# Attention and feed-forward on one core: second phase's layer 2 by seven products of block sums, weight factors partly reloaded, twelve weight halves converted early, V's low parts and the softmax sums on GpSimd

## The chip, the cores and the metric

The kernel runs on one core of one Trainium2 chip. The time is the device time of one execution in microseconds (us); the figure of a kernel is the median of its runs. Engines are named as in the profile: PE is the matrix engine (PEld its weight loads), DVE the vector engine, ACT the scalar engine, POOL GpSimd, SP the engine that issues nearly all DMA transfers.

## The reference

Block-causal attention over 8 batches of 8 heads (576 positions of width 64), followed by a two-layer feed-forward net over the 4608 tokens:

```
scores = where(block_i >= block_j, q @ k^T / 8, -1e9)       # blocks of 64 positions
attn   = softmax(scores);  x = (attn @ v) as [4608, 512]
h      = x @ w_in                                           # [4608, 2048]
g      = max(h, 0) + alpha * min(h, 0)
out    = g @ w_out                                          # [4608, 512]
```

Everything is float32 and the weights come in as float64. A float32 product is made on PE from rounded parts: each operand is split into a high part (its value in PE's float32r format) and a low part (what is left), and three matmuls (high x high, low x high, high x low) are summed in PSUM.

## The kernel before, in words

**A recorded plan.** Every operation is recorded with `op(...)` (L105): engine, an assumed cost, the buffers it reads and writes, a priority. `Plan.schedule` (L133) then runs the whole kernel once with these assumed costs and emits the instructions in the order that comes out, so each engine has one fixed queue. `SHIFTS` (L50) holds hand-set changes of single priorities. Buffers come from rooms of fixed size (`room`, L95) and from quotas by use; a buffer's next user waits until its last user is done. The eight PSUM banks are one such room.

**Attention, about the first 590 us.** There are 32 pairs of heads. `prep` (L730) loads q, k and v of a pair and splits them; from the sixth pair on (`NV` is 5, so for 27 pairs) V is kept as high and low parts: ACT makes the high parts (L764), DVE subtracts to get the low ones (L766). `query_tile` (L832) makes scores of 128 queries, their maximum on DVE, the exponential with its row sum on ACT (L875), adds the two sums of a head on DVE (L879), takes the reciprocal on DVE (L881) and scales the probabilities on POOL (L883); PE transposes them (L891), and they are split again (L970, L971). `values` (L974) multiplies with V. For the split pairs one matmul with 128 stationary columns (high and low part of V side by side) covers two of the three products, a second with 64 columns the third (L1004). The two halves of the result lie in different partitions: ACT copies one out (L1023) and DVE adds it to the other (L1025). The 576 queries of a pair are done as one span of 320 and one of 256.

**Layer work of the first phase.** The hidden width of 2048 is 16 slices of 128. The first `FA` = 6 slices are worked off in chunks of 256 tokens (`chunk_a`, L698) that fill PE between the attention's products, with ordinary products (`ffn1` L574, `ffn2` L606). The sums go to DRAM (`part`).

**Weights.** Float64 halves of a slice (w_in or w_out of 128 hidden units) are made float32 by `to_f32` (L452): one ACT and five DVE passes over 128x512. Four of the twenty halves of the last ten slices are converted during attention (`AHEAD`, L49; `weights_ahead`, L509) and kept in DRAM (`wd`), the rest behind it. `later_weights` (L524) makes, for each two slices, seven block sums of the four quarters of their w_in, split into high and low parts (all sums and low parts on POOL), and splits w_out of each slice.

**Second phase, from about 671 us.** The last ten slices are done in 9 chunks of 512 tokens. `factors` (L626) loads a chunk's x, makes seven block sums of its quarters (four sums and three low parts on DVE, four low parts on POOL). `pair1` (L649) does layer 1 of two slices as seven block products instead of eight, each six matmuls of 128x256 (L660). DVE merges the seven results in PSUM (`plus`, `onto`: L669, L673), and `activate` (L590) makes g for each of the four blocks: ACT (L593), DVE (L595), then the high part on ACT (L599) and the low part on POOL (L602). Layer 2 (`ffn2`, L606) is an ordinary product: for each slice and each 128 tokens three matmuls of 128x512 (L619) into one of four accumulating banks. `store_out` (L1112) adds each bank to the loaded first-phase sum on DVE (L1119) and stores it. So two slices of a chunk, here called a step, take 42 matmuls on L660 and 24 on L619, and there are 5 steps in a chunk and 45 in all. All weight factors of the second phase stay in SBUF.

Of the kernel before, what the change touches and what calls it, by code (L numbers as in the profile page):

```python
# [23 lines left out]
P = 128  # L24
# [13 lines left out]
BANKS, HB, AB, HT, AM, AT, WB = 6, 1, 1, 3, 2, 4, 4  # L38
# [10 lines left out]
AHEAD = {(8 + k // 2, k % 2): 12 + 4 * k for k in range(4)}  # L49
SHIFTS = {  # L50
    9: 2.6, 10: 1.7, 11: -0.8, 12: -0.5, 15: 2.4, 16: 2.1, 19: -5.7, 36: 3.1, 42: 1.1, 59: 0.6, 60: -0.7, 61: 1.4, 81.1574: 2.7, 99: -1,
    101.5278: -0.6, 119.5: 1.1, 121.8981: 0.2, 122.2685: 1.7, 153.5: 1.1, 154.5: 0.3, 155: -0.8, 155.5: 0.8, 156.5: -1.6, 175.2315: 1.4,
    180.4167: -1.6, 184.8611: -3.9,
# [4 lines left out]
B1 = 10  # L58
# [12 lines left out]
IN_ORDER = {"qraw", "kraw", "vraw", "QH", "QL", "KH", "KL", "Q", "K", "V", "raw", "m", "xb", "X", "xt"}  # L71
# [16 lines left out]
class Plan:  # L88
# [16 lines left out]
    def op(self, engine, cost, fn, r=(), w=(), prio=0.0, claim=(), then=None, ends=()):  # L105
# [3 lines left out]
        deps = {j for j, o in enumerate(self.ops) if any(b.kind in ends for b in o[4])} if ends else set()  # L109
# [14 lines left out]
        for b in bufs:  # L124
            b.users += 1
            if b.users == 1 and b.kind in IN_ORDER:
                b.after = self.last.get(b.kind)
                self.last[b.kind] = b
# [4 lines left out]
    def schedule(self):  # L133
# [31 lines left out]
        def lacks(i):  # L165
            need = {}
            for b in self.ops[i][4]:
                if b.slot is None:
                    if b.after and b.after.slot is None:
                        return b.after  # L170
                    need[b.use, b.kind] = need.get((b.use, b.kind), 0) + 1
            for (u, k), v in need.items():
                if self.quota.get(u, 0) < v:
                    return u, None
                if len(self.free.get(k, ())) < v:
                    return None, k
# [145 lines left out]
def attn_ffn(ctx, tc, qT, kT, vT, w_in, w_out, alpha, out):  # L322
# [27 lines left out]
    wd = dram.tile([2 * (NF - FA), P, 512], F32, name="wd")  # L350

# [3 lines left out]
    fa = ExitStack()  # L355
    xring = fa.enter_context(tc.tile_pool(name="xring", bufs=1))
    wa = fa.enter_context(tc.tile_pool(name="wa", bufs=1))
    xT = xring.tile([P, NCC, RING], F32, name="xT")
    fg = ctx.enter_context(tc.tile_pool(name="fg", bufs=1, side="right"))
# [91 lines left out]

    def to_f32(src, prio, after=(), use="att", early=None):  # L452

        raw, eb, fb, mb = Buf("raw"), Buf("bank", use), Buf("bank", use), Buf("m")
# [7 lines left out]
        def e():  # L462
# [14 lines left out]
            r=[raw], w=[fb], prio=prio)  # L477
# [4 lines left out]
            out=mb(), in0=mb(), scalar=2.0 ** -20, in1=eb(), op0=ALU.mult, op1=ALU.mult), r=[eb], w=[mb], prio=prio)  # L482
# [33 lines left out]

    def later(f, i, prio, after=(), use="att"):
        if (f, i) not in AHEAD:
            return to_f32((w_in, w_out)[i][f].bitcast(I32), prio, after, use)
        mb, at = Buf("m"), 2 * (f - FA) + i  # L520
        op("SP", 256, lambda: nc.sync.dma_start(out=mb(), in_=wd[at]), r=[("wd", f, i), *after], w=[mb], prio=prio)
        return mb, mb

    def later_weights(prio):  # L524


        for f in range(FA, NF, 2):
            W = w1s[f] = Buf("w1")

            ms = [later(f + i, 0, *((prio(f), ["att"], "words") if f > FA else (SOON, [], "att"))) for i in range(2)]  # L530
            (m0, w0), (m1, w1) = ms
            sb = Buf("ws")
            q11, q12 = ((m0, lambda j=j, w0=w0: w0()[:, 256 * j:256 * j + 256]) for j in range(2))
            q21, q22 = (((m1, j), lambda j=j, w1=w1: w1()[:, 256 * j:256 * j + 256]) for j in range(2))
            s1, s2 = (((sb, j), lambda j=j, sb=sb: sb()[:, 256 * j:256 * j + 256]) for j in range(2))
            pr = prio(f)
            add("POOL", 256, s1, q21, q22, ALU.add, pr, [m1, "att"])
            add("POOL", 256, s2, s1, q11, ALU.subtract, pr)
            add("POOL", 256, q21, q11, q21, ALU.subtract, pr)
# [634 lines left out]
```

## Time and profile before

| | |
|---|---|
| runs | 1123.67, 1125.45, 1126.57 us; median 1125.45 |
| profiled execution, first to last instruction (its span; the page gives no other time of it) | 1122.8 us |
| busy: PE, DVE, ACT, POOL | 99%, 74%, 64%, 55% of the span |
| instructions on PE | 7288 matmuls, as many weight loads |
| granted PE clock | 1.00 throughout |

The median lies 2.65 us above the span of the profiled execution. Busy time of an engine is the union of its instructions' durations. Instructions that follow each other on DVE overlap a little: the distance from start to start is shorter than a duration. An idle time is put down to the instruction that ended last before the waiting one began.

### The profile page before, as it was taken

How to read it: one execution, taken by the hardware profiler on the slowest of the kernel's cores; microseconds unless marked ns; L12 is line 12 of the kernel's file. 1: busy time of each engine (PE TensorE's matmuls, PEld its weight loads, DVE VectorE, ACT ScalarE, POOL GpSimd, SP SyncE). 2: the span in 40 equal slices, each digit the busy share in tenths (PEclk: the TensorE clock that was granted, in tenths of full speed). 3: DMA queues.
4: the chain of work that ended last, by engine and by line, in shares of the span. 5: the costliest groups of instructions: out<-in, count | busy, mean ns of one | idle time of the engine just before them, and what ended most of it. 6: DMA issues, size and time to landing. Idle time of an engine off the chain costs nothing.

```text
span 1122.8 us, 22035 instructions
## 1 busy us (share of the span) xinstructions
PE 1106.1 (99%) x7288; PEld 988.5 (88%) x7288; DVE 835.2 (74%) x1954; ACT 715.3 (64%) x1933; POOL 613.4 (55%) x769
## 2 busy tenths in 40 slices
PE   8999999999999999999999999999999999999998
PEld 5677989999999999999999888988988998998987
DVE  7888999888888888898857997564647465656554
ACT  7888988888888888788856655343434334343432
POOL 5767556656565556566549987243434334352422
PEclk9999999999999999999999999999999999999999
DMA  8797676576765576567324532221303030312021
GB/s 232 226 261 214 188 221 177 169 201 169 220 170 146 175 191 197 175 170 213 100 93 148 162 101 76 76 72 42 113 1 113 1 114 3 112 38 76 2 75 38
DMA packets 75314, 147.96 MB, mean 132 GB/s; under 512 B 9792, under 2 KB 11840, under 8 KB 75200
## 3 DMA queue, kind: packets, MB, share of 16 engines
q1 hardware_dynamic: 74768, 146.28, 44.4%
q8 instruction: 58, 0.95, 0.4%
q14 instruction: 56, 0.46, 0.1%
q10 hardware_dynamic: 432, 0.27, 0.1%
HBM read 68.40 MB, written 29.36 MB: 87 GB/s over the span
## 4 chain that ended last, share of the span: by engine, by line
PE 85%; DVE 7%; ACT 3%; POOL 2%; issue 2%; DMA 1%; SPq 0%; DVEq 0%; ACTq 0%; POOLq 0%
PE bank L619 33%; PE bank L660 19%; PE bank L582 11%; PE bank L1004 6%; PE bank L859 5%; PE bank L891 5%; PE bank L994 2%; PE bank L921 2%; PE bank L947 1%; ACT p L875 1%; DVE xh L568 1%; PE bank L854 1%; DVE PL L971 1%; DVE g L595 1%; POOL p L883 1%
## 5 line engine op out<-in xcount | busy, mean ns | idle before, releaser
L602 POOL TENSOR_TENSOR gl<-g,gh 128x256 fp32r<-128x256 f32 x288 | 220.0, 772 | 309.6 <-PE bank L660 173.5
L660 PEld LDWEIGHTS bank<-X,w 128*128 128x128 f32 x1890 | 253.7, 189 | 20.6 <-POOL X L488 1.2
L660 PE MATMUL bank<-X,w 128*128 128x256 f32 x1890 | 259.2, 281 | 0.6 <-POOL X L488 0.5
L619 PE MATMUL bank<-w,gh 128*128 128x512 f32 x720 | 225.7, 395 | 1.1 <-DVE g L669 0.7
L883 POOL TENSOR_SCALAR p<-p,ri 128x512 f32<-128x512 f32 (+3 forms) x256 | 153.0, 611 | 115.7 <-DVE ri L881 45.5
L593 ACT ACTIVATE g<-bank 128x256 f32<-128x256 f32 x288 | 110.7, 386 | 155.1 <-DVE bank L673 138.0
L599 ACT CAST gh<-g 128x256 fp32r<-128x256 f32 x288 | 117.0, 407 | 85.2 <-DVE g L595 84.0
L595 DVE SCALAR_TENSOR_TENSOR g<-g,oal,bank 128x256 f32<-128x256 f32 x288 | 136.0, 475 | 42.0 <-ACT g L593 36.6
L673 DVE TENSOR_TENSOR bank<-bank,g 128x256 f32<-128x256 f32 x180 | 76.1, 428 | 104.7 <-PE bank L660 103.2
L875 ACT ACTIVATE p<-bank,nm 128x512 f32<-128x512 f32 (+3 forms) x256 | 135.0, 532 | 20.9 <-DVE nm L872 6.9
L619 PE MATMUL bank<-w,gl 128*128 128x512 f32 x360 | 141.6, 393 | 0.0
L619 PE MATMUL bank<-wa,gh 128*128 128x512 f32 x432 | 140.0, 405 | 0.0
L619 PEld LDWEIGHTS bank<-w,gh 128*128 128x128 f32 x720 | 120.3, 188 | 14.2 <-DVE g L669 0.9
L582 PE MATMUL bank<-xh,wa 128*128 128x256 f32 x864 | 131.2, 287 | 0.4 <-DVE xh L568 0.4
L971 DVE TENSOR_TENSOR PL<-bank,PH 128x512 fp32r<-128x512 f32 (+2 forms) x189 | 111.8, 608 | 12.6 <-ACT PH L970 10.3
L582 PEld LDWEIGHTS bank<-xh,wa 128*128 128x128 f32 x864 | 114.8, 190 | 3.2 <-DVE xh L568 1.1
L891 PE MATMUL bank<-ident,p 128*128 128x128 f32 x640 | 109.4, 276 | 4.7 <-POOL p L883 3.2
L859 PE MATMUL bank<-K,Q 128*128 128x512 f32 (+1 forms) x472 | 104.2, 331 | 0.3 <-ACT p L875 0.2
L970 ACT CAST PH<-bank 128x512 fp32r<-128x512 f32 (+2 forms) x189 | 97.0, 529 | 11.0 <-PE bank L891 7.3
L669 DVE TENSOR_TENSOR g<-bank,g 128x256 f32<-128x256 f32 x135 | 56.8, 422 | 49.1 <-PE bank L660 47.8
L891 PEld LDWEIGHTS bank<-ident,p 128*128 128x128 f32 x640 | 75.3, 140 | 18.6 <-POOL p L883 8.3
L619 PE MATMUL bank<-wa,gl 128*128 128x512 f32 x216 | 85.5, 396 | 0.3 <-POOL gl L602 0.2
(124 smaller groups left out, 2016.7 us busy)
## 6 DMA issues: line engine op xcount, KB each, us to landing
Q<-QH SPq DMA_DIRECT2D x62, 256.0 KB, 3.8
K<-KH SPq DMA_DIRECT2D x124, 128.0 KB, 3.7
vraw<-in_v SPq DMA_DIRECT2D x32, 320.0 KB, 3.1
qraw<-in_q SPq DMA_DIRECT2D x31, 320.0 KB, 3.8
xd<-xT SPq DMA_DIRECT2D x8, 1152.0 KB, 5.7
part<-o SPq DMA_DIRECT2D x36, 256.0 KB, 3.2
xb<-xd SPq DMA_DIRECT2D x9, 1024.0 KB, 5.3
m<-part SPq DMA_DIRECT2D x36, 256.0 KB, 3.3
```

What stands on the lines that cost most here:

```text
L582: nc.tensor.matmul(hp()[:, :n], ww()[:, 0, cc * P:(cc + 1) * P], x()[:, cc, :n], start=(i == 0 and cc == 0), stop=(i == 2 and cc == NCC - 1))
L593: op("ACT", c_act(CHA), lambda: nc.scalar.activation(out=g(), in_=hp()[:, ts], func=AF.Relu, scale=-1.0), r=[hp], w=[g], prio=FP)
L595: op("DVE", c_dve(CHA) + 60, lambda: nc.vector.scalar_tensor_tensor(out=g(), in0=g(), scalar=oal[:, f:f + 1], in1=hp()[:, ts], op0=ALU.mul ...
L599: op("ACT", c_act(CHA, True), lambda: nc.scalar.copy(out=gh(), in_=g()), r=[g], w=[gh], prio=FP)
L602: op("POOL", c_pool(CHA), lambda: nc.gpsimd.tensor_tensor(out=gl(), in0=g(), in1=gh().bitcast(F32), op=ALU.subtract), r=[g, gh], w=[gl], p ...
L619: nc.tensor.matmul(acc(), a()[:, ts], ww(), start=(first and i == 0), stop=(last and i == 2))
L660: nc.tensor.matmul(bank()[:, :CHA], W()[:, i, 256 * at + P * c:256 * at + P * c + P], B()[:, j, CHA * c:CHA * c + CHA], start=(n == 0), st ...
L859: nc.tensor.matmul(o, Q()[:, i, qs], K()[:, 2 * h + i, :w], start=(i == 0), stop=(i == 1))
L875: op("ACT", 238 + w / 1.2, lambda h=h, t=t: nc.scalar.activation(out=t()[:, :w], in_=sb[h]()[:, off[h]:off[h] + w], func=AF.Exp, bias=nm() ...
L883: op("POOL", 244 + w / 1.2, lambda h=h: nc.gpsimd.tensor_scalar(out=pts[h]()[:, :w], in0=pts[h]()[:, :w], scalar1=ri()[:, h:h + 1], scalar ...
L891: nc.tensor.transpose(out=tp()[:, base + c * P:base + (c + 1) * P], in_=pts[h]()[:, c * P:(c + 1) * P], identity=ident)
L971: op("DVE", c_dve(n) + (HALF if n == P else 0), lambda: nc.vector.tensor_tensor(out=lo(), in0=src(), in1=hi().bitcast(F32), op=ALU.subtrac ...
```

## The change

**Layer 2 of the second phase.** `pair2` takes the place of `ffn2` there. For two slices and 256 tokens, the 2x2 blocks of g (two slices by two times 128 tokens) and of w_out (two slices by two times 256 columns) are multiplied with seven block products, each three matmuls of 128x256. g is not split any more when it is made (`activated` writes it to one half of a buffer `G` of 512). Instead `pair2` splits three of its blocks (ACT and POOL, 128x384), makes four block sums in place on DVE (one instruction over two blocks, two over one block each) and splits four blocks (ACT and POOL, 128x512). Four banks take the seven products over all five steps, and `store_out` then merges them with the first-phase sums in seven DVE and four POOL additions of 128x256 and one ACT copy, for 256 tokens. w_out gets block sums and split factors like w_in (`factors_of`); the sums are on DVE now, and of the four low parts of a set two are on DVE and two on POOL.

**Room.** The factors of w_in of four of the five slice pairs (`STREAMED`) share two buffers: each is written to DRAM once (`wq`) and loaded again, 1792 KB, for each of the eight later chunks: 32 loads. Buffers of several kinds now share rooms (x factors, g factors and the first phase's weights; G, x sums and loaded sums). The accumulating banks and the waiting layer-1 results are given more of the eight banks.

**First phase.** Twelve halves instead of four are converted during attention. V's low parts (L766 before) and the addition of the two softmax sums (L879 before) are on POOL. For the span of 256 queries (`LIGHT`) the product of 128 stationary columns becomes two of 64, so all six matmuls of a head end in the same partitions: an ACT copy to xT ends it, and the DVE addition (L1025 before) and the copy L1023 are gone there.

`SHIFTS` is set anew; it is cut below. The order of the changed kernel counts 108 more matmuls of attention (the 108 with 128 stationary columns in the spans of 256 become 216 with 64), 1890 of 128x256 for layer 2 in place of 1080 of 128x512, and 128 sums and 54 low parts of V more on POOL.

Three places in the order. The first is PE in the second phase, in the middle of a chunk. Before (X are x factors, w weight factors, gh and gl the parts of g):

```order
L619 MATMUL bank_181<-w_7878,gh_8159 128x512 x2
L619 MATMUL bank_181<-w_7878,gl_8186 128x512
L660 MATMUL bank_222<-X_7991,w_8230 128x256 x6
L660 MATMUL bank_241<-X_7995,w_8230 128x256 x6
L660 MATMUL bank_188<-X_8118,w_8230 128x256 x6
L619 MATMUL bank_203<-w_8027,gh_520 128x512 x2
L619 MATMUL bank_203<-w_8027,gl_549 128x512
```

In the changed kernel (L705 is layer 1, L785 layer 2; wa are the factors of x and of g, wr a reloaded and w a resident set of weight factors):

```order
L705 MATMUL bank_226<-wa_826,wr_7807 128x256 x6
L705 MATMUL bank_249<-wa_1075,wr_7807 128x256 x6
L785 MATMUL bank_237<-w_8449,wa_7638 128x256 x2
L785 MATMUL bank_237<-w_8449,wa_804 128x256
L785 MATMUL bank_189<-w_7689,wa_370 128x256 x2
L785 MATMUL bank_189<-w_7689,wa_1069 128x256
L705 MATMUL bank_226<-wa_873,wr_7807 128x256 x6
```

All products are now of one size, and a layer-2 product reads factors that ACT, POOL and DVE have made from sums of g.

The second place is DVE in the second phase. Before (u or g are merged results, L595 the activation):

```order
L595 SCALAR_TENSOR_TENSOR g_7465<-g_7465,oal,bank_188 128x256
L673 TENSOR_TENSOR bank_241<-bank_241,g_7445 128x256
L595 SCALAR_TENSOR_TENSOR g_7426<-g_7426,oal,bank_241 128x256
L673 TENSOR_TENSOR bank_222<-bank_222,g_8074 128x256
L669 TENSOR_TENSOR g_7495<-bank_188,g_8074 128x256
```

In the changed kernel (L774, L776, L777 are the block sums of g; L713 and L717 the merges, L725 the activation, L1241 the merge of the sums of layer 2):

```order
L713 TENSOR_TENSOR u_8262<-bank_249,u_8260 128x256
L713 TENSOR_TENSOR u_8099<-bank_237,u_8260 128x256
L774 TENSOR_TENSOR raw_168<-raw_168 128x2x128
L717 TENSOR_TENSOR bank_237<-bank_237,u_8262 128x256
L776 TENSOR_TENSOR raw_168<-raw_168 128x128
L717 TENSOR_TENSOR bank_189<-bank_189,u_8099 128x256
L777 TENSOR_TENSOR raw_168<-raw_168 128x128
L725 SCALAR_TENSOR_TENSOR m_324<-m_324,oal,bank_237 128x256
L1241 TENSOR_TENSOR m_7606<-bank_226,m_7606 128x256
```

Between the merges, which read one operand from a PSUM bank, there now stand sums with both operands in SBUF. One chunk has 106 DVE instructions: 49 merges from PSUM and 20 activations, 30 block sums of g, 4 sums and 3 low parts of x.

The third place is PE in attention, the value product of one head over 256 queries. Before:

```order
L1004 MATMUL bank_181<-PH,V_1236 128x256
L1004 MATMUL bank_181<-PL,V_1236 64x128
L1004 MATMUL bank_181<-PL,V_1236 64x256
L1004 MATMUL bank_181<-PH,V_1236 128x128
```

In the changed kernel:

```order
L1101 MATMUL bank_143<-PH,V_1224 64x256
L1101 MATMUL bank_143<-PH,V_1224 64x128
L1101 MATMUL bank_143<-PH,V_1224 64x256
L1101 MATMUL bank_143<-PH,V_1224 64x128
L1101 MATMUL bank_143<-PL,V_1224 64x256
L1101 MATMUL bank_143<-PL,V_1224 64x128
```

A head has six matmuls there for four.

The diff, cut:

```diff
-AHEAD = {(8 + k // 2, k % 2): 12 + 4 * k for k in range(4)}
+AHEAD = {(10 + k // 2, k % 2): 6 + 2 * k for k in range(12)}
+ON = "DVE", "DVE", "POOL", "DVE", "POOL"
+VLO, SUMS, LIGHT = "POOL", "POOL", (256,)
+STREAMED = (6, 8, 12, 14)
...
 SHIFTS = {
-    9: 2.6, 10: 1.7, 11: -0.8, 12: -0.5, 15: 2.4, 16: 2.1, 19: -5.7, 36: 3.1, 42: 1.1, 59: 0.6, 60: -0.7, 61: 1.4, 81.1574: 2.7, 99: -1,
+    9: 1.6, 11: -0.8, 15: 2.4, 25.5: 2.4, 36: 3.1, 61: 1.4, 63.5: 3.6, 65: -1.3, 66.713: 6, 68.1944: -0.2, 70.0463: 2.5, 72: -1.4, 73.5: -5,
...
+    def factors_of(key, W, m0, m1, sums, pr):
...
+        for to, x, y, f in sums[:3]:
+            to, x, y = ((*q, *t)[k] for k in (to, x, y))
+            add(ON[0], 256, to, x, y, f, pr, [b0, b1, "att"])
+        for src, r, at, n in ((w0, [b0, "att"], 0, 512), (w1, [b1], 2, 512), (lambda: sb(), [t[0][0], t[1][0]], 4, 512)):
...
+            split(src, hi, lo, n, [*r, *[(r[0], j) for j in range(2) if at < 4]], ((*key, at), "h"), ((*key, at), "l"), [W], ON[1 + at // 2], pr)
...
+    def weights_of(f):
...
+        W = Buf("wr")
+        op("SP", 1792, lambda: nc.sync.dma_start(out=W().rearrange("p a b -> p (a b)").bitcast(F32), in_=wq[STREAMED.index(f)]),
+           r=[("wq", f)], w=[W], prio=0)
...
+    def pair2(f, G, accs, turn, tail):
...
+        def parts(j, n, src):
+            op("ACT", c_act(n * T, True), lambda: nc.scalar.copy(out=at(0, j, n), in_=src()), r=gk, w=[(F[0], j)], claim=F, prio=turn)
+            on = "DVE" if j and tail else "POOL"
...
+        parts(0, 3, lambda: g(1, 3))
+        op("DVE", c_dve(2 * T), lambda: nc.vector.tensor_tensor(out=blocks(2, -2 * T), in0=blocks(0, 0), in1=blocks(2, -T), op=ALU.subtract),
+           w=gk, prio=turn)
+        op("DVE", c_dve(T), lambda: nc.vector.tensor_tensor(out=g(1), in0=g(1), in1=g(2), op=ALU.subtract), w=gk, prio=turn)
+        op("DVE", c_dve(T), lambda: nc.vector.tensor_tensor(out=g(3), in0=g(3), in1=g(1), op=ALU.subtract), w=gk, prio=turn)
+        parts(3, 4, lambda: g(0, 4))
...
+                for n, (x, y) in enumerate(((0, 0), (0, 1), (1, 0))):
+                    nc.tensor.matmul(accs[bank]()[:, 256 * half:256 * half + 256], at(x, j), W()[:, y, w:w + 256],
+                                     start=(first and n == 0 and not half), stop=(last and n == 2), skip_group_check=True)
...
-                op("DVE", c_dve(n), lambda cs=cs: nc.vector.tensor_tensor(
+                op(VLO, c_pool(n) if VLO == "POOL" else c_dve(n), lambda cs=cs: (nc.gpsimd if VLO == "POOL" else nc.vector).tensor_tensor(
...
+            if SUMS == "POOL":
+                op("POOL", 130, lambda: nc.gpsimd.tensor_tensor(out=sp(), in0=s()[:, :, 0], in1=s()[:, :, 1], op=ALU.add),
...
+                if q1 in LIGHT:
+                    prods = [(x, c) for c, _ in cs for x in ("h", "m", "l")]
...
+    def store_out(accs, t):
...
+        op("ACT", c_act(256), lambda: nc.scalar.copy(out=u1(), in_=acc(0)), r=[accs[0]], w=[u1], prio=FP)
+        plus(lambda: half(ohi, 0), lambda: acc(1), lambda: half(ohi, 0), [accs[0]], [(ohi, 0)])
+        plus(lambda: half(ohi, 0), lambda: half(ohi, 0), u1, [u1], [(ohi, 0)], "POOL")
+        plus(u2, lambda: acc(3), u1, [accs[1], u1], [u2])
...
     fs = range(FA, NF, 2)
-    for t0 in range(0, TOK, CHB):
+    for c, t0 in enumerate(range(0, TOK, CHB)):
         X = factors(t0)
...
+        gs = [pair1(f, X, base + L1T * i) for i, f in enumerate(fs)]
+        for k in range(2):
+            accs = [Buf("bank", "acc") for _ in range(4)]
+            for i, f in enumerate(fs):
...
+                pair2(f, gs[i][k], accs, turn2, t0 + CHB == TOK)
+            store_out(accs, t0 + CHA * k)
```

252 lines of the change are left out of this document (161 added, 91 removed), and 8 rows, old and new, of the table SHIFTS.

## The prediction

> **What bounds the kernel now.** First the page's totals, the granted clock and the chain that ended last.
>
> ```profile
> PE 1106.1 (99%) x7288; PEld 988.5 (88%) x7288; DVE 835.2 (74%) x1954; ACT 715.3 (64%) x1933; POOL 613.4 (55%) x769
> ...
> PEclk9999999999999999999999999999999999999999
> ...
> PE 85%; DVE 7%; ACT 3%; POOL 2%; issue 2%; DMA 1%; SPq 0%; DVEq 0%; ACTq 0%; POOLq 0%
> ```
>
> PE is idle for 1122.8 - 1106.1 = 16.7 us and always at full clock, so a gain needs less PE work, and a loss needs an engine that makes PE wait. The windows (PE, PEld, DVE, ACT, POOL busy, clock, DMA share, GB/s) show where the others stand.
>
> ```profile
> 200.00:300.00 100.00, 99.83 (x720) 92.88 (x719) 88.19 (x226) 83.85 (x243) 61.45 (x82) 1.00 0.67 187
> ...
> 650.00:670.00 20.00, 18.95 (x120) 16.46 (x120) 19.96 (x41) 10.68 (x27) 17.24 (x18) 1.00 0.23 75
> ...
> 700.00:800.00 100.00, 100.00 (x627) 89.88 (x626) 57.97 (x125) 39.93 (x99) 41.03 (x47) 1.00 0.19 64
> ```
>
> In attention DVE at 88% costs PE 0.2%. Behind it, while weights are made, DVE is busy 99.8% of 20 us and PE loses 1.05 us, 5%. In the second phase DVE and POOL have room. The chain of waits gives PE's prices there (start, time, what).
>
> ```profile
> 700.04 2.79 PE bank L619 x12
> 702.84 2.12 PE bank L660 x18
> ...
> 710.57 2.81 PE bank L619 x12
> ```
>
> 2.79/12 = 0.2325 us for 512 columns, 2.12/18 = 0.1178 for 256. A step is 24 x 0.2325 + 42 x 0.1178 = 10.53 us, just what lies between the starts at 700.04 and 710.57: nothing but matmuls fill it.
>
> **Layer 2 by seven products.** It takes 1080 x 0.2325 = 251.1 us now and will take 1890 x 0.1178 = 222.6: -28.5 us. The price is that of layer-1 products, which have the same form. A chunk of 512 tokens is then 420 x 0.1178 = 49.5 us of PE, for 52.7.
>
> **The value products.** One head over 256 queries, from PE's timeline:
>
> ```profile
> 304.90 0.28 PE L1004 MATMUL bank<-PH,V 128*128 128x256 f32 x1
> 305.02 0.34 PE L1004 MATMUL bank<-PL,V 128*64 128x128 f32 x2
> 305.19 0.23 PE L1004 MATMUL bank<-PH,V 128*128 128x128 f32 x1
> 305.25 0.83 PE L891 MATMUL bank<-ident,p 128*128 128x128 f32 x6
> ```
>
> From start to start the 256-wide one takes 0.12 us and the 128-wide one 0.06. Two more are added: 0.18 x 54 = +9.7 us, on PE, which is full there, so all of it counts. That the halved weight loads give something back would show as short intervals behind the 64-column ones, and 305.02 to 305.19 (0.17 for 256 and 128) shows none.
>
> **Engines in attention.** The groups by form (busy, mean ns):
>
> ```profile
> L766 DVE TENSOR_TENSOR V<-vraw,V 128x384 fp32r<-128x384 f32 x27 | 17.3, 642 | 3.5 <-ACT V L764 3.2
> L766 DVE TENSOR_TENSOR V<-vraw,V 128x256 fp32r<-128x256 f32 x27 | 12.5, 463 | 0.0
> L879 DVE TENSOR_REDUCE sp<-s 128x2 f32<-128x4 f32 x128 | 19.1, 150 | 11.1 <-ACT p L875 9.9
> L1025 DVE TENSOR_TENSOR xT<-bank,tmp 64x256 f32<-64x256 f32 x54 | 22.6, 418 | 2.9 <-ACT tmp L1023 1.9
> L478 DVE SCALAR_TENSOR_TENSOR m<-raw,bank 128x512 f32<-128x512 uint32 x32 | 21.6, 679 | 0.0
> L570 POOL TENSOR_TENSOR xl<-xT,xh 128x384 fp32r<-128x384 f32 x8 | 8.3, 1047 | 1.1 <-DVE xh L568 0.7 <-PE bank L582 0.4
> L602 POOL TENSOR_TENSOR gl<-g,gh 128x256 fp32r<-128x256 f32 x288 | 220.0, 772 | 309.6 <-PE bank L660 173.5 <-ACT gh L599 123.0 <-PE bank L619 10.3
> L883 POOL TENSOR_SCALAR p<-p,ri 128x128 f32<-128x128 f32 x64 | 28.2, 451 | 11.0 <-DVE ri L881 6.8 <-ACT KH L746 1.1 <-ACT xT L1012 1.1
> ```
>
> DVE loses 17.3 + 12.5 + 19.1 + 22.6 = 71.5 us and gets eight more conversions, 8 x 5 x 0.68 = 27. POOL gets 27 x (1.05 + 0.77) = 49 us of low parts and 128 sums. A sum of 128x2 is not in the trace on POOL: between 0.15 us (DVE's, with nothing for POOL's start) and 0.45 (its 128x128 form); I take 0.25, so 32 us. POOL goes from about 60% to 75% over some 580 us, DVE down to about 80%. Both stay below what DVE carries at 88% now: zero in the sum. The sum waits in POOL's queue behind a low part of up to 1 us, and behind it wait the reciprocal, the scaling and the transposes; chunk work of the first phase fills PE meanwhile. Without that cover it would be 128 x up to 1 us. A gain on PE is excluded by its 99.8%. The sixteen DMAs of eight conversions (512 KB in, 256 KB out) meet a DMA share of 0.67: nothing.
>
> **Engines in the second phase.** This decides. The price of POOL's wide forms and of DVE's narrow one, and DVE's timeline in a stretch where POOL runs without a break, then POOL's own:
>
> ```profile
> L488 POOL TENSOR_TENSOR w<-m,w 128x512 fp32r<-128x512 f32 x20 | 26.3, 1318 | 3.3 <-ACT w L487 3.3
> L971 DVE TENSOR_TENSOR P<-bank,P 64x128 fp32r<-64x128 f32 x27 | 7.7, 284 | 1.7 <-ACT P L970 0.8
> ```
>
> ```profile
> 736.97 1.11 DVE L488 TENSOR_TENSOR X<-xt,X 128x512 fp32r<-128x512 f32 x1
> 738.00 0.47 DVE L595 SCALAR_TENSOR_TENSOR g<-g,oal,bank 128x256 f32<-128x256 f32 x1
> 738.39 0.41 DVE L669 TENSOR_TENSOR g<-bank,g 128x256 f32<-128x256 f32 x1
> 738.72 1.06 DVE L504 TENSOR_TENSOR xt<-xb,xt 128x512 f32<-128x512 f32 x1
> 739.70 1.23 DVE L488 TENSOR_TENSOR X<-xt,X 128x512 fp32r<-128x512 f32 x1
> ...
> 750.34 0.68 DVE L488 TENSOR_TENSOR X<-xb,X 128x512 fp32r<-128x512 f32 x1
> 750.94 0.88 DVE L673 TENSOR_TENSOR bank<-bank,g 128x256 f32<-128x256 f32 x2
> ```
>
> ```profile
> 736.23 3.00 POOL L488 TENSOR_TENSOR X<-xb,X 128x512 fp32r<-128x512 f32 x2 [1.83 <-ACT X L487]
> 739.20 1.18 POOL L602 TENSOR_TENSOR gl<-g,gh 128x256 fp32r<-128x256 f32 x1
> 740.34 1.74 POOL L488 TENSOR_TENSOR X<-xb,X 128x512 fp32r<-128x512 f32 x1
> ```
>
> Start to start, DVE takes 0.39 us for an activation, 0.33 for a 256-wide merge, 0.60 for a 512-wide sum (750.34 to 750.94). But a DVE instruction with both operands in SBUF takes 0.68 us alone and 1.11, 1.06 and 1.23 while POOL works: 0.45 us longer on average. POOL is slowed as well (1.74 for 1.32). A merge with one operand in PSUM (738.39) is not.
>
> POOL per chunk: ten splits of 384 and ten of 512, eight additions, four low parts of x: 10 x 1.05 + 10 x 1.32 + 8 x 0.77 + 4 x 1.32 = 35.2 us, 71% of 49.5. DVE per chunk: 49 x 0.33 + 20 x 0.39 + 10 x (0.33 + 0.28 + 0.28) + 7 x 0.60 = 37.1 us. Of these, 37 instructions have both operands in SBUF; at 0.45 x 0.71 = 0.32 us each they wait 11.8 us. DVE comes to 48.9 us, 99% of PE's time. ACT has 0.39 of its time in use and trades four splits of 256 for two pairs of wider ones: no bound.
>
> By the Trainium skill (SBUF — State Buffer, Who interferes with whom) the two engines share a port that the second comer does not get until the first one's instruction ends, when a DVE instruction has two SBUF inputs and POOL reads SBUF. The trace agrees: 1.23 us against 0.68.
>
> So the change spends nearly all of DVE's room. The cost to PE lies between nothing and the 5% of the window with DVE at 99.8%: 0 to 23 us of 446. I take 7, nearer the lower end, since products of both layers fill in for each other and PE lost only 0.2% at 88%.
>
> **The making of the weights.** Eight conversions fewer stand behind attention (-27 us of DVE); ten sets of sums and low parts on DVE, 10 x (4 x 0.33 + 2 x 0.60) = +25 us, and their six SBUF instructions wait on POOL, up to 60 x 0.32 = 19 us. POOL is freed: five sets of 0.77 x 4 + 1.32 x 3 + 0.77 and ten single splits of 1.32, 52 us, become 10 x (1.32 + 0.77) = 21. Between -1 and +8 us on PE (5% of the 150 us in question); I take +1.
>
> **Reloads.** 32 loads of 1792 KB. From the page's issues:
>
> ```profile
> xb<-xd SPq DMA_DIRECT2D x9, 1024.0 KB, 5.3
> m<-part SPq DMA_DIRECT2D x36, 256.0 KB, 3.3
> ```
>
> The 768 KB between these cost 2.0 us, so 1792 KB land in 5.3 + 2.0 = 7.3 us, or 9.3 in proportion to the larger. In the order 87 to 102 matmuls, 10.3 to 12.0 us, stand between the last use of the old set and the first of the new for half the loads, some 20 us for the rest. They are hidden: zero.
>
> **The end.** The last 256 tokens need a POOL addition (0.77) behind DVE's, and whole stores instead of halves: +1.2 us.
>
> Sum: -28.5 + 9.7 + 7 + 1 + 1.2 = -9.6 us. The span goes from 1122.8 to 1113.2; with the 2.65 us between the span and the median of the runs, 1115.8. Without any new wait it would be 1107.8, with the 23 us it would be 1131.8.
>
> **The rivals.** *DVE becomes the bound* (slower). If the mean wait of the 37 instructions passes (49.5 - 37.1)/37 = 0.335 us, DVE and not PE sets the chunk. POOL's instructions get longer (1.05 and 1.32 for 0.77), and half of one is 0.59 us; times 0.71 that is 0.42, so 52.6 us a chunk, +3.1 x 9 = 28 us instead of 7: 1137. At 0.45, POOL always busy, it is 53.8 and 1147. For it: the sums are back to back with waits on each other, so POOL's next instruction can slip in between each two. Against it: 0.32 is below the point, and in attention a DVE nearly as full costs nothing. By the rule of the Trainium skill quoted above (SBUF — State Buffer, Who interferes with whom) the wait is the rest of POOL's instruction, and the time that of this rival.
>
> *The making of the weights stalls PE.* The DVE work there grows by up to 17 us net; if PE pays 8, the time is 1123, no change. For it: DVE is at 99.8% there already. Against: POOL's 31 us less.
>
> *The reloads come late* (slower). If they land after 12.5 us, because x, sums and stores share the queues, 16 of them cost 1.5 us each: +24, 1140. Against: 10.5 MB a chunk (four reloads, x, sums, stores) in 49.5 us is 212 GB/s, and the window at 200 us moves 187 at a share of 0.67 with smaller packets.
>
> *The saving is not there*, because the products of layer 2 don't run at 0.1178: the count is set by the order and the form is that of layer 1, so this is unlikely.
>
> **How the numbers follow.** A measurement can tell about 0.3% (3.4 us) from no change: faster is below 1122.1, slower above 1128.8. Forecast 0.57 (own range 1107 to 1123), DVE as the bound 0.24, weights 0.11, reloads 0.06, no saving 0.02. Faster: 0.54 of the forecast and 0.05 of the weights, 0.59. Same: 0.03, 0.05 of the weights, 0.06 of the milder cases of DVE, 0.14. Slower: the rest, 0.27. The range goes from 1106 to 1142: it leaves out DVE's upper cases (0.08), half the reloads (0.03) and little below.
>
> **What would show it.** Right: layer 2 at 0.118 us a matmul and PE at 98% or more in the second phase; DVE near full there, with the sums of g (128x2x128) lengthened to 0.6 us or more; chunks 50 to 51 us apart. Attention longer by 10 us. Wrong: chunks 52.5 us or more apart with PE waiting for DVE or POOL (the rival), PE waiting for a DMA into wr (reloads), PE below 95% between 600 and 750 us (weights).

## The result, and the profile after

| | before | after |
|---|---|---|
| median of the runs | 1125.85 us (1123.67 to 1126.57, 4 runs) | 1185.22 us (1183.0 to 1185.7, 4 runs) |
| ratio | | 1.0529, 95% interval 1.0514 to 1.0544 |
| span of the profiled execution | 1122.8 us | 1181.2 us |

The change costs 59 us; 9.6 us of gain were forecast. The page of the changed kernel:

```profile
PE 1110.8 (94%) x8206; PEld 1027.7 (87%) x8206; DVE 972.7 (82%) x2147; ACT 732.7 (62%) x1961; POOL 762.6 (65%) x983
...
PEclk9999999999999999999999979999999999999999
...
PE 64%; DVE 23%; issue 5%; ACT 3%; POOL 3%; DMA 1%; SPq 0%; POOLq 0%; DVEq 0%; ACTq 0%
```

PE is busy about as long as before, but the chain runs through DVE for 23% of the span, not 7%, and one slice of the clock is below 9. The windows tell where (PE, PEld, DVE, ACT, POOL busy, clock, DMA share, GB/s; in parentheses the instructions):

```profile
200.00:300.00 100.00, 97.87 (x720) 91.09 (x721) 80.70 (x185) 84.24 (x245) 70.67 (x115) 1.00 0.71 206
597.00:653.00 56.00, 55.75 (x354) 50.60 (x355) 50.40 (x83) 30.77 (x70) 37.27 (x35) 1.00 0.56 209
653.00:713.00 60.00, 43.45 (x289) 39.47 (x288) 58.32 (x108) 29.03 (x67) 31.03 (x27) 0.86 0.49 171
713.00:773.00 60.00, 53.51 (x420) 51.41 (x420) 51.96 (x109) 23.09 (x54) 36.30 (x33) 0.97 0.47 176
773.00:1046.00 273.00, 259.17 (x2159) 255.49 (x2158) 235.80 (x541) 117.36 (x279) 179.40 (x165) 1.00 0.55 202
1096.00:1181.00 85.00, 70.78 (x564) 67.71 (x564) 66.47 (x146) 27.45 (x65) 40.24 (x41) 0.99 0.28 103
```

Read PE's column against the length of each row. Attention is nearly full. In the first chunk of the second phase, while weights are still made, PE stands for 16.6 of 60 us beside a DVE that is busy for 58.3. In the steady chunks (773 to 1046) all products are 256 wide, so the count of matmuls tells the loss: 2159 x 0.1178 = 254.3 us of work in 273, 18.7 us or 6.8% lost, although DVE is busy for only 86%.

The whole by stages. "Lost" is the length of a stage less its matmuls at 0.2325 or 0.1178 us each; the stages are cut at the first layer-1 product of a chunk.

| | before | after | difference |
|---|---|---|---|
| first layer-1 product of the second phase | 641.8 | 653.0 | +11.2 |
| lost in chunks 1 and 2 | 3.2 | 35.5 | +32.3 |
| lost in chunks 3 to 8 | 0 | 25.8 | +25.8 |
| lost in chunk 9 | 0 | 13.4 | +13.4 |
| behind the last matmul | 3.7 | 5.4 | +1.7 |
| work of PE (what is left) | | | -26.0 |
| span | 1122.8 | 1181.2 | +58.4 |

What works on DVE and POOL in the steady chunks, by form (busy us, mean ns of one | idle before it). The group rows here and below are of 773 to 1070 us, the window rows of 773 to 1046; the sums that use the second buffer (`raw`, 15 of each) are rows of their own and are left out:

```profile
L717 DVE TENSOR_TENSOR bank<-bank,u 128x256 f32<-128x256 f32 x111 | 44.7, 421 | 7.7 <-ACT m L723 4.3 <-PE bank L705 3.5
L774 DVE TENSOR_TENSOR m<-m 128x256 f32<-128x256 f32 x41 | 30.0, 732 | 4.7 <-POOL wa L771 4.7
L776 DVE TENSOR_TENSOR m<-m 128x128 f32<-128x128 f32 x41 | 23.6, 576 | 0.4
L777 DVE TENSOR_TENSOR m<-m 128x128 f32<-128x128 f32 x41 | 17.5, 427 | 0.4
L771 POOL TENSOR_TENSOR wa<-m,wa 128x512 fp32r<-128x512 f32 x40 | 52.9, 1325 | 49.2 <-ACT wa L769 41.3 <-issue 4.1 <-PE bank L705 2.3
```

The merge with one operand in PSUM (L717) and the block sum with both in SBUF (L774) have one size: 0.42 and 0.73 us. The two smaller sums differ by 0.15 us though they are the same instruction. POOL has its price of before (1.32) and is idle for 49 us before these low parts, 41 of them for ACT. ACT in turn waits for DVE's last sum, and PE for DVE's activation (us, times, longest), in the same stretch:

```profile
POOL wa L771 <- ACT wa L769: 68.1, 41, 4.0
ACT wa L769 <- DVE m L777: 58.9, 26, 4.8
...
PE bank L705 <- DVE m L725: 6.8, 6, 1.6
```

The chain of waits inside a steady chunk (start, time, what) is a row of DVE instructions, and the lengthened sums stand in it:

```profile
850.15 0.52 ACT wa L769
850.99 0.87 DVE m L725 x2
851.86 0.34 DVE bank L717
852.20 0.89 DVE m L774
853.11 1.14 DVE m L776
```

Of the other steps, the reloads and what attention gave to POOL:

```profile
wr<-wq SPq DMA_DIRECT2D x32, 1792.0 KB, 7.3
```

```profile
L859 POOL TENSOR_TENSOR V<-vraw,V 128x384 fp32r<-128x384 f32 x27 | 27.4, 1013 | 24.4 <-ACT V L857 20.4 <-DMA K<-KH 3.5 <-POOL sp L973 0.3
L973 POOL TENSOR_TENSOR sp<-s 128x2 f32<-128x2 f32 x128 | 25.6, 203 | 50.6 <-ACT p L968 50.2
```

No DMA into wr stands among PE's waits. A sum of 128x2 costs POOL 0.20 us.

### The profile page after: what moved, and what is told of

Same layout as the page of the kernel before. It is cut to its first block, busy times and chain, and to the rows that moved or that the text cites. A ratio compares the mean times of both kernels' runs of the same rounds, so it can differ in the third digit from the quotient of the medians.

```text
span 1181.2 us, 24258 instructions
## 1 busy us (share of the span) xinstructions
PE 1110.8 (94%) x8206; PEld 1027.7 (87%) x8206; DVE 972.7 (82%) x2147; ACT 732.7 (62%) x1961; POOL 762.6 (65%) x983
## 4 chain that ended last, share of the span: by engine, by line
PE 64%; DVE 23%; issue 5%; ACT 3%; POOL 3%; DMA 1%; SPq 0%; POOLq 0%; DVEq 0%; ACTq 0%
PE bank L624 12%; PE bank L661 10%; PE bank L705 9%; PE bank L785 9%; PE bank L1101 7%; PE bank L952 6%; PE bank L988 5%; DVE bank L717 2%; DVE u L713 2%; DVE m L774 2%; DVE m L519 2%; PE bank L1091 2%; PE bank L1018 2%; DVE m L776 1%; POOL wa L771 1%
## 5 line engine op out<-in xcount | busy, mean ns | idle before, releaser
L785 PE MATMUL bank<-w,wa 128*128 128x256 f32 x1890 | 269.6, 285 | 19.7 <-POOL wa L771 9.2
L785 PEld LDWEIGHTS bank<-w,wa 128*128 128x128 f32 x1890 | 243.8, 191 | 25.4 <-POOL wa L771 12.6
L705 PE MATMUL bank<-wa,wr 128*128 128x256 f32 x1512 | 215.1, 285 | 24.9 <-DVE m L725 12.2
L705 PEld LDWEIGHTS bank<-wa,wr 128*128 128x128 f32 x1512 | 195.2, 192 | 30.8 <-DVE m L725 14.5
L771 POOL TENSOR_TENSOR wa<-m,wa 128x384 fp32r<-128x384 f32 (+1 forms) x125 | 148.1, 1195 | 104.6 <-ACT wa L769 91.0
L980 POOL TENSOR_SCALAR p<-p,ri 128x256 f32<-128x256 f32 (+3 forms) x256 | 140.7, 562 | 34.8 <-DVE ri L978 30.6
L968 ACT ACTIVATE p<-bank,nm 128x256 f32<-128x256 f32 (+3 forms) x256 | 134.1, 530 | 23.2 <-DVE nm L965 11.8
L644 POOL TENSOR_TENSOR gl<-g,gh 128x256 fp32r<-128x256 f32 x108 | 86.2, 798 | 50.0 <-ACT gh L641 43.2
L1067 ACT CAST PH<-bank 128x512 fp32r<-128x512 f32 (+2 forms) x189 | 96.9, 528 | 17.2 <-PE bank L988 12.9
L965 DVE TENSOR_REDUCE nm<-bank 128x1 f32<-128x384 f32 (+1 forms) x128 | 76.7, 616 | 11.1 <-PE bank L952 9.9
L1101 PE MATMUL bank<-PH,V 128*128 128x320 f32 (+3 forms) x432 | 85.1, 289 | 0.0
L771 POOL TENSOR_TENSOR wa<-raw,wa 128x384 fp32r<-128x384 f32 (+1 forms) x45 | 54.4, 1213 | 44.7 <-ACT wa L769 36.1
L717 DVE TENSOR_TENSOR bank<-bank,u 128x256 f32<-128x256 f32 x180 | 71.9, 422 | 13.2 <-PE bank L705 7.2
```

What stands on the lines that cost most here:

```text
L705: nc.tensor.matmul(bank()[:, :CHA], W()[:, i, 256 * at + P * c:256 * at + P * c + P], B()[:, j, CHA * c:CHA * c + CHA], start=(n == 0), st ...
L771: op(on, c_pool(n * T) if on == "POOL" else c_dve(n * T), lambda: (nc.gpsimd if on == "POOL" else nc.vector).tensor_tensor(out=at(1, j, n) ...
L785: nc.tensor.matmul(accs[bank]()[:, 256 * half:256 * half + 256], at(x, j), W()[:, y, w:w + 256], start=(first and n == 0 and not half), st ...
L968: op("ACT", 238 + w / 1.2, lambda h=h, t=t: nc.scalar.activation(out=t()[:, :w], in_=sb[h]()[:, off[h]:off[h] + w], func=AF.Exp, bias=nm() ...
L980: op("POOL", 244 + w / 1.2, lambda h=h: nc.gpsimd.tensor_scalar(out=pts[h]()[:, :w], in0=pts[h]()[:, :w], scalar1=ri()[:, h:h + 1], scalar ...
L1067: op("ACT", c_act(n) + (HALF if n == P else 0), lambda: nc.scalar.copy(out=hi(), in_=src()), r=rk, w=[(*k, 0) for k in wk], prio=pr)
```

## The experiments

Theory A, formed after the result: a DVE instruction with two SBUF operands waits for POOL's running instruction; these waits lengthen the chain from g to the factors in every chunk, and fill DVE while the weights are made. Rival B: the longer chain itself (activation, split, sums, split) is too long for the order, waits or not. Rival D: the reloads. All times below stand against runs of the kernel before on the same chip (1124.3 to 1125.1 us). The first four experiments keep the order of the changed kernel. In all others it is made anew, with the `SHIFTS` that were set by hand for the changed kernel, so a part of their differences can be the order's.

**One SBUF input for the sums of g.**

```
-tensor_tensor(out=g(1), in0=g(1), in1=g(2), op=ALU.subtract)
+tensor_reduce(out=g(1), in_=g(1) with an axis of 1, axis=AX.X, op=ALU.add)     # and so for all three
```

> The three block sums of g in pair2 (L774, L776, L777) are replaced by DVE passes of the same length in the same order that read one operand from SBUF instead of two, so that they don't ask for what POOL holds; the subtraction is left out, so layer 2 multiplies other numbers. Nothing else moves. Theory A (DVE's two-input instructions wait for POOL, and these waits delay the factors): these instructions fall to 0.42 and 0.28 us each, the six steady chunks lose 1 us instead of 4.3, the last 80 us lose half, 1185 becomes about 1150. Theory B (the chain merge, activation, split, three sums, split is too long and DVE too full even without waits): 1178 to 1190, chunks still 53 us apart.

Measured: 1147.0 us (ratio 1.0199, 1.0169 to 1.0228), 38 less than the changed kernel. The windows, then the groups of the steady chunks:

```profile
653.00:773.00 120.00, 101.64 (x740) 96.24 (x739) 105.56 (x221) 55.55 (x129) 70.57 (x63) 0.90 0.51 184
773.00:1046.00 273.00, 272.04 (x2301) 271.03 (x2301) 218.06 (x585) 125.86 (x298) 188.46 (x177) 1.00 0.58 217
```

```profile
L775 DVE TENSOR_REDUCE m<-m 128x128 f32<-128x128 f32 x88 | 23.1, 275 | 0.0
L775 DVE TENSOR_REDUCE m<-m 128x256 f32<-128x256 f32 x44 | 18.0, 410 | 2.1 <-POOL wa L771 2.1
```

The subtraction is left out; the order, the sizes and POOL's work are the same. 0.41, 0.275 and 0.275 us stand where 0.73, 0.58 and 0.43 stood, and PE loses 273 - 2301 x 0.1178 = 1.9 us instead of 18.7. B falls. The Trainium skill (SBUF — State Buffer, Who interferes with whom) says that a tensor_reduce never contends with GpSimd on trn2, and that at most one SBUF input, outside DVE's 2-port modes, keeps DVE off the shared port; these rows agree.

**The same for all sums and for DVE's low parts of x and of the weights** (not for the low parts of g that DVE makes in the last chunk).

> As the run before, and also the sums of x and of the weights and the low parts that DVE makes read one SBUF operand only, in the same order (subtractions left out). Theory A: the waits are gone everywhere, the 35 us lost between 653 and 773 us fall below 12, total about 1120. Theory B: as without this, 1175 to 1190. Theory C (behind attention DVE has simply too much to do to make the weights in time, waits or not): the chunks behind 773 us get as in the run before, but 25 us or more stay lost between 653 and 773 us, total 1135 to 1150.

Measured: 1122.56 us (ratio 0.9976, 0.9965 to 0.9987).

```profile
653.00:773.00 120.00, 113.77 (x914) 111.33 (x913) 99.01 (x269) 62.96 (x149) 79.19 (x76) 0.97 0.63 228
773.00:1046.00 273.00, 273.00 (x2321) 273.00 (x2320) 210.50 (x583) 128.23 (x300) 184.83 (x177) 1.00 0.57 208
```

The steady chunks are now full, and chunks 1 and 2 lose 10.8 us instead of 35.5. So the waits are worth 62.7 us of 1185, and without them the change would just about break even. The run takes POOL's waits for DVE away as well; they are small, since POOL's low parts of g shrink only from 1.33 to 1.30 us (512 columns) and from 1.07 to 1.02 (384). In chunks 1 and 2 the sums of g alone (the run before) bring 4.8 of the 24.7 us, the sums and low parts of the weights and of x the rest. Theory C of this expectation (DVE has too much to do there, waits or not) falls: 10.8 us are lost, not 25 or more.

**The other side of the conflict: little work for POOL.** The low parts of g's factors on 16 columns:

```
-out=at(1, j, n), in0=src(), in1=at(0, j, n)
+out=at(1, j, n)[:, :16], in0=src()[:, :16], in1=at(0, j, n)[:, :16]
```

> The low parts of g's factors (384 and 512 columns) are written for 16 columns only, the rest is left out; every other instruction and the order stay. This takes GpSimd's side of the conflict away and leaves VectorE's sums with their two SBUF operands. Theory A (VectorE waits for GpSimd's instruction to end): GpSimd falls from 65% to some 30% of the steady chunks, the sums from 0.73, 0.58 and 0.43 us to at most 0.50, 0.38 and 0.35, and the chunks lose 0-1 us: 1130-1150 us. Rival W (the sums are long of themselves, because they read and write one buffer in place): 0.73, 0.58 and 0.43 us stay, and the time falls only by what the shorter GpSimd instructions take out of the chain: 1160-1180 us.

Measured: 1142.96 us (ratio 1.0159, 1.0143 to 1.0175). Window and groups of the steady chunks:

```profile
773.00:1046.00 273.00, 270.42 (x2289) 269.65 (x2288) 222.96 (x582) 123.83 (x293) 86.35 (x175) 1.00 0.57 211
```

```profile
L774 DVE TENSOR_TENSOR m<-m 128x256 f32<-128x256 f32 x43 | 22.9, 532 | 0.0
L776 DVE TENSOR_TENSOR m<-m 128x128 f32<-128x128 f32 x43 | 14.5, 338 | 1.7 <-DVE m L774 0.5
L777 DVE TENSOR_TENSOR m<-m 128x128 f32<-128x128 f32 x44 | 13.5, 306 | 0.4
```

The sums are unchanged in code, yet take 0.53, 0.34 and 0.31 us with POOL busy for 32% instead of 66%. So their length is POOL's doing; rival W falls. (L774 stays 0.03 us above what was expected at most.) This run shortens the chain as well, so its time alone would not tell A from B; the durations do.

**Reloads of 64 bytes** in each partition instead of the whole set:

```
-dma_start(out=W()..., in_=wq[...])
+dma_start(out=W()...[:, :16], in_=wq[...][:, :16])
```

> The 32 reloads of weight factors move 16 of the 3584 words of each partition; issues, waits and order stay (the factors of the reloaded sets are mostly those of another slice). Theory D (reloads come late or their traffic slows others): 15 us faster or more. Theories A, B and C: within 4 us of 1185, since PE's waits in the trace name DVE, POOL and ACT, and the reloads land in 7.3 us.

Measured: 1184.46 us (ratio 1.0532, 1183.94 to 1184.98 us): no change. D falls.

**A version with the whole computation and no wait at the sums of g.** ACT copies g into a PSUM bank, and each sum reads one operand there:

```
+op("ACT", ..., nc.scalar.copy(out=C(), in_=g(0, 4)), r=gk, w=[C], claim=F)       # C = Buf("bank", "gp"), one
-tensor_tensor(out=g(1), in0=g(1), in1=g(2), op=ALU.subtract)
+tensor_tensor(out=g(1), in0=c(1), in1=g(2), op=ALU.subtract)                     # and so for all three
```

> Before the three block sums of g, ScalarE copies g into one PSUM bank (one more buffer, taken from the eight) and each sum reads one of its two operands there: one SBUF input for each of the three, the computation whole. Theory A (time lost to VectorE's waits): the sums take 0.40-0.45 and 0.28 us instead of 0.75, 0.57 and 0.41, the steady chunks lose 0-2 us instead of 4.3, and the weights stage loses less: 1145-1162 us. Rival L (what counts is the length of the chain from g to the factors, whoever makes it long): the copy adds 0.6 us to a chain from which 0.76 us of waits go, and one bank fewer holds the merges: 1172-1190 us.

Measured: 1158.26 us (ratio 1.0296, 1.028 to 1.0311). Window and groups of the steady chunks:

```profile
773.00:1046.00 273.00, 266.00 (x2203) 261.65 (x2202) 216.64 (x560) 144.17 (x332) 184.18 (x168) 1.00 0.56 203
```

```profile
L783 DVE TENSOR_TENSOR m<-bank,m 128x256 f32<-128x256 f32 x40 | 16.8, 420 | 4.7 <-ACT bank L782 2.8 <-POOL wa L771 1.1
L786 DVE TENSOR_TENSOR m<-bank,m 128x128 f32<-128x128 f32 x41 | 11.8, 287 | 0.9
L785 DVE TENSOR_TENSOR m<-bank,m 128x128 f32<-128x128 f32 x41 | 11.7, 285 | 0.5
```

The sums are as short as A said, with POOL as busy as ever (184 of 273), and 27 us come back. But 2203 x 0.1178 = 259.5: the steady chunks still lose 13.5 us of 273. The time lies in A's range, but two thirds of what the waits cost there are still lost, some 2.5 us a chunk, above A's 0-2. So rival L is right in part: the length of the chain counts too. Which costs more, the copy in the chain, the bank less or the new order on ACT and DVE, was not separated.

**Who makes the weights.** First all on POOL (`ON` five times "POOL"):

> All block sums of the weights and all their low parts on GpSimd, as the kernel before had them; the plan is made anew. In the changed kernel VectorE is busy 58.3 of the 60 us from 653 to 713, and the first two chunks of the second phase lose 35.5 us of TensorE's time. Theory A (VectorE, stretched by its waits for GpSimd, sets the pace while the weights are made): some 28 us of VectorE's instructions leave 597 to 773 and about 32 us come onto GpSimd, which was busy 67 of the 120 us there: the loss falls to 10-20 us, 1165-1178 us. Rival C (the number of sums and splits is too much for either engine in this time): GpSimd is over 90% busy in that stretch and the loss stays at 30 us or more, 1180-1200 us. The six steady chunks lose their 25 us under both.

Measured: 1192.35 us (ratio 1.0596, 1.058 to 1.0612).

```profile
653.00:713.00 60.00, 28.21 (x196) 26.20 (x195) 20.21 (x42) 24.18 (x53) 59.69 (x63) 0.76 0.49 170
```

Now POOL is full (59.7 of 60) and PE stands for 32 us. Rival C's marks came true (chunks 1 and 2 lose 39.5 us): giving DVE's part back only changes which engine is full. That the work is too much for either engine holds for POOL; DVE, freed of its waits, could do it in time (the run with all sums on one input). Then, on top of the PSUM copy, the low parts of both raw halves on POOL, where one of them and that of the last sum are already; the block sums and the low parts of the first two sums stay on DVE (`ON = "DVE", "POOL", "POOL", "DVE", "POOL"`):

> The PSUM copy of g, and the weights' work split between the two engines: block sums and the low parts of the sums on VectorE, the low parts of the raw halves on GpSimd; the computation whole. In the version with the PSUM copy alone VectorE is busy 55.6 of the 60 us from 653 to 713 and GpSimd 32.8; with all on GpSimd it is 59.7 against 20.2. Theory A with C (whichever engine is full sets the pace of the making, and the sum of both leaves room): about 45 us on each, the two first chunks lose 4-9 us instead of 14: 1148-1155 us. Rival (the order of the conversions and the DMA, not an engine, sets the pace): no change, 1156-1162 us.

Measured: 1157.78 us (ratio 1.0294, 1.0275 to 1.0312), no change to the PSUM copy alone.

```profile
653.00:713.00 60.00, 44.01 (x304) 39.85 (x302) 55.79 (x106) 33.07 (x75) 46.08 (x37) 0.91 0.50 174
```

My 45 us on each engine did not come: POOL rises to 46.1 while DVE stays at 55.8, now for 106 instructions (with the PSUM copy alone 55.6 us for 112): what is left on DVE takes longer beside a busier POOL. The rival's range (1156 to 1162) holds the time; the split is not the cure. The 14 us of my expectation were wrong as well: counted as in the table above, chunks 1 and 2 lose 27.8 us with the PSUM copy alone and 23.9 here, and 3.0 of these 3.9 us go again because the second phase starts later.

**Early conversions undone**: four halves in attention, as many as before (`for k in range(4)` in `AHEAD`; slices and places are not those of the kernel before).

> Four weight halves converted early in attention, as the kernel before had it, not twelve; the other eight are converted between attention and the second phase; the plan is made anew. Theory A with C (VectorE is full while the weights are made: 160.7 of the 176 us from 597 to 773): eight conversions are 32 VectorE instructions of 0.68 us, 22 us, which come on top of that; attention ends some 0-4 us earlier, the second phase's first two chunks lose 45-60 us instead of 35.5: 1192-1210 us. Rival R (the early conversions are what makes attention longer, and the later place has room): attention's last product by 592 us instead of 597.4, no more lost behind it: 1176-1186 us.

Measured: 1198.32 us (ratio 1.066, 1.0632 to 1.0688). Attention's last product is at 593.6 us instead of 597.4; chunk 3 begins at 786.2 instead of 773.3. The early conversions cost attention about 4 us and have saved 13 on balance by chunk 3; chunks 1 and 2 lose 47.8 us without them. That is what A with C expected.

**Attention.** `LIGHT = ()`, so the span of 256 is multiplied as before:

> LIGHT is emptied: value products, copies and additions of the spans of 256 as before the change, the order planned anew. By the prediction's term PE has 9.7 us less to do in attention; if the 64-column products also cause the 7 us that PE loses there (it waits for ACT copies behind them), attention ends 15 to 17 us earlier, total 1168 to 1172; if that loss comes from POOL's added work (V's low parts, softmax sums), only 8 to 10, total 1175 to 1178. A DVE that gets 22 us more could cost some of it again.

Measured: 1178.99 us (ratio 1.0483, 1.043 to 1.0537), above both expectations; attention's last product is at 593.0 instead of 597.4, 4.4 us earlier where 8 to 17 were expected. The two runs took 1176.55 and 1181.44 us, and the interval overlaps that of the changed kernel (1.0514 to 1.0544): the gain of 6 us is not clear of noise. And V's low parts and the softmax sums back on DVE (`VLO, SUMS = "DVE", "DVE"`):

> V's low parts and the softmax sums back on VectorE, all else as changed; the plan is made anew. The changed kernel's attention is 17.2 us longer on TensorE, of which 9.7 are the products that give up a cheaper form. Theory P (the other 7.5 us are waits for what went to GpSimd in attention): the second phase starts some 5-8 us earlier, 1177-1181 us. Rival Q (they come of the early conversions and the new order): no change or worse, 1184-1192 us, the second phase's first product at 652-660 us.

Measured: 1192.67 us (ratio 1.0604, 1.0586 to 1.0622); attention's last product at 600.3, the second phase's first at 666.0. P falls: undoing what went to POOL there gains nothing. Q's marks (1184 to 1192 us, first product at 652 to 660) were missed too, by 0.7 and 6 us on the slow side.

**Together**: PSUM copy, weights on POOL, no LIGHT.

> The PSUM copy of g, all weight sums and low parts on GpSimd, and no products in the dearer form in attention, together; the computation whole. Theory A: 38 us of waits in the steady chunks, up to 20 us in the weights stage and 6 us in attention go, less the copy's cost: 1115-1145 us. Rivals L and C: the chain stays as long and GpSimd is too full to make the weights in time: 1165-1190 us.

Measured: 1167.8 us (ratio 1.0378, 1.0362 to 1.0393). That is in the range of rivals L and C and 9.5 us slower than the PSUM copy alone, with POOL busy for 53 of the 60 us from 653 to 713 and PE for 27.7: the work on POOL outweighs what leaving LIGHT out can give. No version with the whole computation beat the kernel before.

## Why the prediction was wrong, step by step

- *Layer 2, -28.5.* Right. The price of 0.1178 us holds (2321 matmuls in 273 us without waits), and the 1890 products of layer 2 ran at it. PE's work behind the first layer-1 product fell by 26.0 us and not by 28.5, because twelve first-phase products of 512 columns (12 x 0.2325 = 2.8 us) now run behind it.
- *DVE waits for POOL.* The mechanism was right and its size nearly so: 0.32 us a wait were forecast; the three sums are 0.32, 0.30 and 0.15 us longer than with one input, 0.26 on average. POOL's 71% was 66%, DVE's 99% was 86%.
- *"I take 7, nearer the lower end, since products of both layers fill in for each other."* This step failed. It put the cost down to DVE's share of busy time, capped by the 5% of one window at 99.8%. PE lost 6.8% with DVE at 86%, because the chain from g to the factors now has two splits and three sums in it, each waiting in one queue behind merges for the other product; a wait of 0.26 us on each sum delays all that is queued behind it. Chunks 3 to 9 lost 39 us; chunks 3 to 8 are 51.2 to 57.2 us long, five of the six above 52.5, the mark that the prediction set for DVE as the bound. The rival "DVE becomes the bound" had the same flaw: its point of decision, a mean wait of 0.335 us, was not reached, and the loss came all the same. The attention row misled (DVE at 88%, PE loses 0.2%): there first-phase products can fill gaps, which is the likely reason and was not tested. It was also a favourable row: in the 100 us before it DVE is busy for 90% and PE loses 1.8%.
- *The making of the weights, +1 (-1 to +8).* The step that failed by most: +32 us in chunks 1 and 2. The rival of that name had the place and the engine right and the price, 8 us, wrong. Both took 5% of PE as the most that a full DVE can cost, from one window of 20 us (650 to 670). That window was second phase already (it began at 641.8 us, not at about 671 as said ahead) and held no first-phase products, so missing filler does not tell the two stages apart. From 653 to 713 PE loses 28% beside a DVE full for nearly 60 us. PE's waits from 653 to 773, 22.9 us in all (us, times, longest), are mostly for g:

```profile
PE bank L785 <- POOL wa L771: 6.8, 7, 1.7
PE bank L705 <- DVE m L725: 4.1, 4, 1.9
PE bank L705 <- DVE wr L503: 3.3, 1, 3.3
```

  Only the last of these rows is one for weights. The chain of g shares its engines with the making of the weights, and it is now longer by the sums. Removing all waits of DVE takes 24.7 of the 35.5 us away, 20 of them with the sums and low parts of weights and x; with all of the weights' work on POOL that engine is full. Why the kernel before lost only 5% beside a full DVE was not tested.
- *LIGHT, +9.7.* Counted from start to start without idle time, the value products of the spans of 256 went from 21.7 to 36.1 us, +14.4, while the transposes of both kinds fell from 73.9 to 70.9. PE's timeline shows how:

```profile
308.43 0.27 PE L988 MATMUL bank<-ident,p 128*128 128x128 f32 x1
308.46 0.36 PE L1101 MATMUL bank<-PH,V 128*64 128x256 f32 x1
308.66 0.27 PE L988 MATMUL bank<-ident,p 128*128 128x128 f32 x1
308.69 0.36 PE L1101 MATMUL bank<-PL,V 128*64 128x256 f32 x1
```

  A light product and a transpose take 0.23 us together, nearly all of it at the light one. So 9.7 was too little for the products themselves, and the claim that nothing comes back failed; the two errors cancel in part, and that the net of 11.4 is near 9.7 is luck. Left out, attention ends only 4.4 us earlier: the first-phase products up to there take 264.8 us instead of 257.9, with 1585 of them for 1581. Why was not found; a stretch at lower granted clock (0.57 from 296 to 300 us of that trace) is a part of it.
- *Engines in attention, zero.* Attention's last product is 17.2 us later (580.2 to 597.4). LIGHT accounts for 4 and the early conversions for 4, each taken out alone; V's low parts and the sums on POOL for none; each trial also makes the order anew. PE's own account in the two traces, counted the same way, assigns the 17.2 us: value products +13.7 (both spans), transposes -3.0, twelve more first-phase products +1.2, other products +0.4, and idle time +4.9 (9.7 to 14.6). So the zero failed by 4.9 us. With the early conversions undone 3.1 of them are gone; the rest stays open. The second phase's first product is only 11.2 us later.
- *Reloads, zero.* Right: 7.3 us to landing, as forecast, and small reloads change nothing.
- *The end, +1.2.* It was 1.7, but chunk 9, which has no next chunk's layer 1 beside it, lost 13.4, where 3.4 are left in the run with one input; the forecast had no term for that.

The sum of the terms without any new wait was 1107.8 in the forecast; the run without the waits gives 1122.56. So even with the waits' cost set right, the forecast would have been 15 us low, 16 by the spans: some 7.6 from the weights (10.8 - 3.2; the +1 is not in 1107.8), 4 from the end (1.7 + 3.4 - 1.2), 2 from the start of the second phase (653.8 - 641.8 - 9.7) and 2.5 from the first-phase products that now run behind that start.

## What to carry to other kernels

An engine at 86% can still cost the matrix engine 7%, if its instructions stand in the chain that feeds the next product: cost the chain, not the share. Before putting an elementwise step with two SBUF operands on DVE beside a busy GpSimd, add a wait to each. GpSimd's share times half its mean instruction is an estimate that came out on the high side twice: 0.66 x 0.54 = 0.36 us in the changed kernel (mean 179.4/165 = 1.09), where 0.26 was measured, and 0.32 x 0.25 = 0.08 with 16 columns (mean 86.35/175 = 0.49), where it was 0.07. Look for a form with one operand in PSUM. And a loss read from 20 us of one stage is no bound for another: 5% there became 28% here.

## What the runs showed of the hardware

The wait falls faster than POOL's share: with the sums' code unchanged, POOL at 32% instead of 66% and with mostly short instructions, the excess over the one-input durations fell from 0.32, 0.30 and 0.15 us to 0.12, 0.06 and 0.03. And a long stall costs PE twice, as idle time and in the products behind it. From the windows, and from PE's timeline (both of the changed kernel):

```profile
680.00:700.00 20.00, 12.30 (x67) 10.93 (x68) 19.80 (x36) 8.96 (x21) 10.46 (x10) 0.66 0.53 181
682.00:695.00 13.00, 6.64 (x26) 5.46 (x26) 12.79 (x24) 5.73 (x14) 6.63 (x6) 0.50 0.55 215
705.40:708.20 2.80, 2.78 (x14) 2.78 (x15) 2.67 (x4) 1.22 (x4) 1.12 (x1) 0.55 1.02 435
```

```profile
705.42 2.74 PE L785 MATMUL bank<-w,wa 128*128 128x256 f32 x12 [2.76 <-DVE m L725]
707.96 1.38 PE L705 MATMUL bank<-wa,wr 128*128 128x256 f32 x6
```

With PE starved the granted clock is 0.66 over 20 us and 0.50 from 682 to 695. Behind a further wait it is 0.55, and twelve matmuls of 256 take 707.96 - 705.42 = 2.54 us, 0.21 each instead of 0.118. The Trainium skill (TensorE: Matmul & The Clock Gate, Part 1) says that the clock drops to half after an idle window; the row of 0.50 agrees. In chunks 1 and 2, 57 products start in such stretches of low clock; an estimate from their distances is that this makes up some 7 of the 35.5 us lost there.
